# Another order table for a scan-plus-MLP kernel on one core: same operations, other turns, 39 table loads instead of 43

## The chip, the core and the metric

The kernel runs on one core of a Trainium2 chip. A core has five engines that each work through their own list of instructions in order: TensorE (PE in the rows; PEld are its weight loads), VectorE (DVE), ScalarE (ACT), GpSimd (POOL) and SyncE (SP), which here only issues DMAs. They wait for each other through semaphores. The metric is the device time of one execution in microseconds (us); lower is better. The median of three runs before the change is 571.08 us.

## The reference

```
for t in range(S):                                   # S = 768, for 4 x 8 heads, D = 48
    ar, ai = (a_re_n[:, :, t, :, None], a_im_n[:, :, t, :, None])
    new_re = ar * S_re - ai * S_im
    new_im = ar * S_im + ai * S_re
    kv = np.einsum('bhd,bhe->bhde', k[:, :, t], v[:, :, t])
    S_re, S_im = (new_re + kv, new_im)
    y[:, :, t] = np.einsum('bhd,bhde->bhe', q[:, :, t], S_re)
```

Here a_re_n and a_im_n are a_re and a_im, scaled so that their magnitude stays under 0.999. The result y, as 3072 rows of 384, goes through a two-layer MLP: h = x @ w_in (384 to 2048), g = h * tanh(softplus(h)), out = g @ w_out (2048 to 384), all in float32.

## The kernel before

**Tiling.** The 768 time steps of the 4 batches are cut into 12 units of 256 steps, each of two chunks of 128. The recurrence is computed chunk by chunk with matmuls. A unit goes through three stages.

- *Elementwise* (`ew_steps`): magnitudes and phases of the decay, with logarithm, exponential, sine and arctangent on ACT, scans and products on DVE, then `X` and `QK` (the k and q that carry the decay) are sent through DMA into the tile `T`, with head dimensions on the partitions.
- *Attention* (`attn_steps`): for each chunk the masked products of q and k (`amat`: matmuls into `pa` or `pp`, DVE masks them into `am`), the transposed k (`kn`: matmuls into `pkn`, or a DVE transpose and a DMA in later units), the output `yv` (matmuls into `ypsum` from `am` and v, and from `T` and the state `S`) and the new state `upd` (matmuls into `pd` or `pp`, DVE adds and scales into `S`). ACT copies `ypsum` into `y`, and DMAs bring it into `xf`, from which come the high and low parts `xH` and `xL`.
- *MLP* (`moe_steps`): eight steps a unit. `mm1` makes `ph`, 18 matmuls of 256 columns (two halves of nine); then ACT, DVE, ACT, ACT, ACT, DVE turn it into `g`, which is split into `gh` and `gl`; `mm2` adds 12 matmuls of 384 columns to `po`. At the end of a unit DVE scales `po` into `o`, and a DMA writes it out.

Beside these stand the loading and splitting of the weights (`raw`, `wx`, `w`) and 84 matmuls on a constant, `junk` (L516), 40 of which wait for the first phase on DVE and 44 for the first copy of `y`; they compute nothing that is used.

**Column widths.** A matmul of `ph`, `po`, `pa`, `pkn` and `junk` works on the full 128 columns of the array. Those of `ypsum` (L603, 48 output rows) and of `pd` in units 0 to 2 (L623) work in a half of 64 columns, those of `pp` (L583 for the masked products, L623 for the state, from unit 3 on) in a strip of 32. In TensorE's order these widths follow each other in runs; a place where one matmul has another width than the one before it is called a turn here.

**Order.** The code is written once, in a plan of due times; the tables in `ORDER` then fix the order of every engine's instructions. A table lists numbers of instructions in the order in which the code made them; `a+n` stands for n of them from a on. `in_order` chains each engine's instructions by its table. ACT's functions lie in two sets of tables, one for logarithm and exponential ("l"), one for sine and arctangent ("t"); `SETS` lists the loads (L240), which the ACT table then places.

```
    for engine, text in ORDER.items():
        ...
        for run in text.split():
            first, _, count = run.partition("+")
            for n in range(int(first), int(first) + int(count or 1)):
                if last is not None:
                    tc.add_manual_dep(own[n], last.name, order, reason="order of the engine")
                last = own[n]
```

At the end a check value `total` is summed over the partitions by one small matmul, `ptotal` (L809); DVE makes the flag `okay` of it, and every engine reads the flag and, where it is set, skips a general path that this input never takes.

Of the kernel before, what the change touches and what calls it, by code (L numbers as in the profile page):

```python
# [117 lines left out]
    """,  # L118
    "DVE": """
# [51 lines left out]
    """,  # L171
    "Pool": """
        14 3+2 1 16 0 15 2 5+6 55 11+3 17 19 18 20+3 24 23 26 25 27+6 35 33+2 37+2 36 39+2 42 41 43+6 50 49 52 51 54
        53
    """,
    "SP": """
# [12 lines left out]
    """,  # L189
}  # L190

SETS = "l t l t l t l t l t l t l t l t l t l t l t l t l t l t l t l t l t l t l t l t l t l"

# [793 lines left out]
```

## Time and profile before

| What | Value |
|---|---|
| runs | 570.53, 571.08, 571.2 us; median 571.08 |
| the profiled execution's span | 570.8 us |
| PE busy | 545.7 us (96%) |
| DVE busy | 474.2 us (83%) |
| ACT busy | 467.9 us (82%) |
| POOL busy | 43.1 us (8%) |
| chain that ended last, by engine | PE 71%, DVE 11%, ACT 10%, DMA 4% |
| ACT table loads | 43, 1283 ns each |

The span of the profiled execution stands 0.3 us under the median of the runs. Busy shares are averages over the whole span: at the start PE waits for data and DVE works, in the middle both are busy, and after some 300 us DVE and ACT have idle time while PE has none. Matmuls are pipelined, so that one is shown with some 0.28 us while the next one starts after 0.12; what a matmul takes of PE's time is the distance from its start to the next one's.

### The profile page before, as it was taken

How to read it: one execution, taken by the hardware profiler on the slowest of the kernel's cores; microseconds unless marked ns; L12 is line 12 of the kernel's file. 1: busy time of each engine (PE TensorE's matmuls, PEld its weight loads, DVE VectorE, ACT ScalarE, POOL GpSimd, SP SyncE). 2: the span in 40 equal slices, each digit the busy share in tenths (PEclk: the TensorE clock that was granted, in tenths of full speed). 3: DMA queues.
4: the chain of work that ended last, by engine and by line, in shares of the span. 5: the costliest groups of instructions: out<-in, count | busy, mean ns of one | idle time of the engine just before them, and what ended most of it. 6: DMA issues, size and time to landing. Idle time of an engine off the chain costs nothing.

```text
span 570.8 us, 14397 instructions
## 1 busy us (share of the span) xinstructions
PE 545.7 (96%) x5830; PEld 507.6 (89%) x5830; DVE 474.2 (83%) x793; ACT 467.9 (82%) x749; POOL 43.1 (8%) x59
## 2 busy tenths in 40 slices
PE   0789999999999999999999999999999999999996
PEld 0367777789999999999999999999999999999996
DVE  5989999999999998989887999886799787545543
ACT  7889899799979898998988997798987967545671
POOL 4021313431000000000000010000000000000000
PEclk9979999999999999999999999999999999999999
DMA  8666874815563755705647508617524615201001
GB/s 297 218 174 217 279 248 139 265 51 149 164 174 108 218 178 144 211 16 166 170 133 208 161 21 220 199 34 191 160 73 130 210 51 149 75 7 53 1 15 45
DMA packets 69063, 81.65 MB, mean 143 GB/s; under 512 B 6144, under 2 KB 60672, under 8 KB 68992
## 3 DMA queue, kind: packets, MB, share of 16 engines
q1 hardware_dynamic: 68992, 80.68, 48.0%
q8 instruction: 47, 0.77, 0.5%
q14 instruction: 24, 0.20, 0.1%
HBM read 45.51 MB, written 11.40 MB: 100 GB/s over the span
## 4 chain that ended last, share of the span: by engine, by line
PE 71%; DVE 11%; ACT 10%; DMA 4%; issue 2%; SPq 1%; DVEq 0%; ACTq 0%
PE ph L690 27%; PE po L727 27%; PE ypsum L603 6%; PE pp L583 3%; ACT L240 2%; PE po L723 2%; PE pp L623 2%; PE junk L516 2%; DMA T<-QK 1%; DVE X L419 1%; DVE g L700 1%; DMA raw<-w_in 1%; PE ph L686 1%; ACT e L697 1%; ACT e L694 1%
## 5 line engine op out<-in xcount | busy, mean ns | idle before, releaser
L690 PE MATMUL ph<-xH,w 128*128 128x256 f32 x1104 | 215.7, 286 | 0.1
L727 PE MATMUL po<-w,gh 128*128 128x384 f32 x704 | 193.0, 338 | 0.0
L690 PEld LDWEIGHTS ph<-xH,w 128*128 128x128 f32 x1104 | 177.4, 191 | 3.3 <-issue 1.2
L690 PE MATMUL ph<-xL,w 128*128 128x256 f32 x552 | 156.5, 284 | 0.0
L727 PEld LDWEIGHTS po<-w,gh 128*128 128x128 f32 x704 | 127.4, 188 | 1.2 <-issue 0.6
L727 PE MATMUL po<-w,gl 128*128 128x384 f32 x352 | 118.1, 337 | 0.0
L690 PEld LDWEIGHTS ph<-xL,w 128*128 128x128 f32 x552 | 105.2, 191 | 0.9 <-DVE xL L249 0.2
L700 DVE SCALAR_TENSOR_TENSOR g<-e,ph 128x512 f32<-128x512 f32 (+1 forms) x100 | 65.7, 659 | 32.2 <-ACT e L698 31.0
L696 ACT ACTIVATE e<-e 128x512 f32<-128x512 f32 (+1 forms) x100 | 60.7, 610 | 38.5 <-DVE e L695 38.2
L694 ACT ACTIVATE e<-ph 128x512 f32<-128x512 f32 (+1 forms) x100 | 57.1, 574 | 28.9 <-PE ph L690 17.1
L727 PEld LDWEIGHTS po<-w,gl 128*128 128x128 f32 x352 | 66.1, 188 | 0.1
L249 DVE TENSOR_TENSOR gl<-g,gh 128x512 fp32r<-128x512 f32 x88 | 60.1, 685 | 6.9 <-ACT gh L248 6.4
L695 DVE TENSOR_SCALAR e<-e 128x512 f32<-128x512 f32 (+1 forms) x100 | 40.9, 411 | 28.7 <-ACT e L694 28.5
L698 ACT ACTIVATE e<-e 128x512 f32<-128x512 f32 (+1 forms) x100 | 61.0, 612 | 1.8
L697 ACT ACTIVATE e<-e 128x512 f32<-128x512 f32 (+1 forms) x100 | 60.9, 612 | 1.8
L240 ACT ACT_TABLE_LOAD x43 | 55.2, 1283 | 1.5 <-PEq L941 0.8
L516 PE MATMUL junk<-cmask 128*128 128x512 bf16 x84 | 24.9, 445 | 14.4 <-DVE I L425 14.4
L283 POOL TENSOR_TENSOR raw<-raw 128x768 int32<-128x768 int32 x16 | 27.8, 1747 | 84.4 <-DVE raw L281 37.7
L603 PE MATMUL ypsum<-T,S 96*48 96x128 f32 x320 | 32.1, 276 | 0.2 <-DVE S L631 0.2
L516 PEld LDWEIGHTS <-cmask 128*128 128x128 bf16 x84 | 9.1, 111 | 25.8 <-issue 20.6
L248 ACT CAST gh<-g 128x512 fp32r<-128x512 f32 x40 | 24.4, 610 | 4.7 <-DVE g L700 2.5
L584 DVE COPY_PREDICATED am<-tmask,pp 128x512 f32<-128x512 uint8 x36 | 26.0, 734 | 1.3 <-PE pp L583 1.2
(101 smaller groups left out, 839.0 us busy)
## 6 DMA issues: line engine op xcount, KB each, us to landing
T<-X SPq DMA_DIRECT2D x72, 129.0 KB, 2.6
T<-QK SPq DMA_DIRECT2D x72, 129.0 KB, 2.6
raw<-w_in SPq DMA_DIRECT2D x8, 768.0 KB, 7.1
raw<-w_out SPq DMA_DIRECT2D x8, 768.0 KB, 7.6
kd<-vx SPq DMA_DIRECT2D x45, 128.0 KB, 2.9
kn<-kd SPq DMA_DIRECT2D x15, 384.0 KB, 3.1
V<-v SPq DMA_DIRECT2D x12, 384.0 KB, 4.6
out_dram<-o SPq DMA_DIRECT2D x24, 192.0 KB, 2.6
```

The source lines that it names most:

```text
L240: nc.scalar.preload_act_table_set({"l": "natural_log_exp_and_others", "t": "trig_and_small"}[name])
L249: leng(out=lo, in0=src, in1=h.bitcast(F32), op=ALU.subtract)
L516: ins = nc.tensor.matmul(junk, cmask, cmask.unsqueeze(1).broadcast_to([P, 4, P]), start=True, stop=True)
L603: nc.tensor.matmul(py[64 * par:64 * par + D, i, :], lhs, rhs, start=n == 0, stop=first or n == 1)
L690: nc.tensor.matmul(ph[:, a, :], rows_in(parts[j][:, wp], kt, a), st[xp][:, kt, :], start=n == 0, stop=n == 8)
L694: act(e, ph, AF.Exp)
L695: nc.vector.tensor_scalar_min(e, e, math.exp(20.0))
L696: act(e, e, AF.Square, bias=1.0)
L697: act(e, e, AF.Ln, scale=0.2, bias=0.2)
L698: act(e, e, AF.Exp, scale=-1.0)
L700: nc.vector.scalar_tensor_tensor(g, e, 2.5, ph, ALU.subtract, ALU.mult)
L727: nc.tensor.matmul(po[t], gp[:, a, tsl], rows_out(parts[NPAIR + j][:, wp], a), start=j in starts and a == 0 and n == 0, stop=j + 1 in ends ...
```

## The change

Only the tables change: the order of the instructions of all five engines (`ORDER`) and the list of table loads (`SETS`), 43 before and 39 after. One line fewer moves every line below by one: L516 is L515 in the changed kernel. Of the tables one line each is shown.

```
 ORDER = {
     "PE": """
-        0+20 48+4 40+4 52+4 20+2 56+4 44+4 60+15 22+13 124+4 75+5 128+2 35 132+4 130 188+6 36+2 226+3 38 80+5 136+4 85
+        0+26 40+4 26+2 48+4 28+2 44+4 30+2 56+4 32+2 52+4 64+16 34 60+4 80+5 35 85 36 86+2 124+8 88+5 132+4 93+2 37
...
-SETS = "l t l t l t l t l t l t l t l t l t l t l t l t l t l t l t l t l t l t l t l t l t l"
+SETS = "l t l t l t l t l t l t l t l t l t l t l t l t l t l t l t l t l t l t l t l"
```

In TensorE's order the number of turns between widths goes from 103 to 97, by kind: wide to narrow (from 128 columns to 64 or 32) 39 and 39, narrow to wide 39 and 38, from 32 to 64 columns 11 and 16, from 64 to 32 columns 14 and 4. Runs of `ph` are now cut at multiples of nine and runs of `po` at multiples of three, and there are more changes between these two, both 128 columns wide: 147 before, 221 after. `ptotal`, before ahead of the last 54 matmuls of `po`, now stands behind them. Of the 84 junk matmuls 20 stood ahead of the first matmul on data, now 26; behind the two runs of `ypsum` of the first chunk stood 62, now 49.

**VectorE, the first chunk.** `am` are the two masked tiles of the first chunk, `S` is the first state, `raw` and `wx` weights; the number behind a name tells tiles apart. Before:

```order
L590 TENSOR_TENSOR am_384<-pa_383,cmask_83 128x512
L397 TENSOR_SCALAR X_296<-X_296 128x3x128 x2
L376 TENSOR_TENSOR I_202<-I_202,X1_295 128x384
L398 SCALAR_TENSOR_TENSOR R_201<-X_296 128x384 x2
L402 SCALAR_TENSOR_TENSOR R_201<-rmask_96,R_201 128x384 x2
L281 SCALAR_TENSOR_TENSOR raw2_170<-raw2_170,wx2_413 128x768
L376 TENSOR_TENSOR I_202<-I_202,X1_295 128x384
L452 TENSOR_SCALAR cnt_234,good_146<-QK_156 128x3
L280 TENSOR_SCALAR wx3_448<-raw3_174 128x768
L628 TENSOR_TENSOR S_428<-pd_429,T_212 96x384
L590 TENSOR_TENSOR am_516<-pa_515,cmask_83 128x512
```

And now:

```order
L589 TENSOR_TENSOR am_380<-pa_379,cmask_83 128x512
L627 TENSOR_TENSOR S_424<-pd_425,T_208 96x384
L396 TENSOR_SCALAR X_292<-X_292 128x3x128
L375 TENSOR_TENSOR I_198<-I_198,X1_291 128x384
L279 TENSOR_SCALAR wx2_409<-raw2_166 128x768
```

The state now follows directly on the second mask; before, eight rows of elementwise and weight work stood between them, and the next chunk's first mask came directly behind the state.

**TensorE, the same place.** `pa` are the products that the masks read, `pkn` the transposed k, `pd` the products that the state reads. Before:

```order
L603 MATMUL ypsum_142<-am_343,V_184 48x128 x4
L552 MATMUL pkn_330<-ident_78,T_212 128x96 x4
L603 MATMUL ypsum_142<-am_384,V_184 48x128 x4
L623 MATMUL pd_429<-V_184,kn_144 64x48
L623 MATMUL pd_429<-V_184,kn_144 33x48
```

And now:

```order
L602 MATMUL ypsum_138<-am_339,V_180 48x128 x4
L515 LDWEIGHTS cmask_83
L515 MATMUL junk_250<-cmask_83 128x512
L515 LDWEIGHTS cmask_83
L515 MATMUL junk_250<-cmask_83 128x512
L587 MATMUL pa_379<-T_208 128x128 x4
L622 MATMUL pd_425<-V_180,kn_140 64x48
```

The matmuls of the state (16, in turns of 64 and 33 output rows) now stand together ahead of the second run of `ypsum`; before, 11 of them stood behind it, and the other five behind 13 junk matmuls and four of `pkn`. ACT's copies of `pkn` into `kn`, which they read, stand ahead of a table load that they followed before.

**TensorE, the first visit to 32 columns (unit 3).** `pp` from `T` are masked products, `pp` from `V,kn` the state's. Before:

```order
L623 MATMUL pp<-V,kn 32x48 x24
L603 MATMUL ypsum<-am,V 48x128
L603 MATMUL ypsum<-am,vx 48x128 x2
L603 MATMUL ypsum<-am,vz 48x128
L603 MATMUL ypsum<-am,V 48x128
L603 MATMUL ypsum<-am,vx 48x128 x2
L603 MATMUL ypsum<-am,vz 48x128
L583 MATMUL pp<-T 32x128 x4
```

And now:

```order
L582 MATMUL pp<-T 32x32 x4
L622 MATMUL pp<-V,kn 32x48 x24
L602 MATMUL ypsum<-am,V 48x128
L602 MATMUL ypsum<-am,vx 48x128 x2
L602 MATMUL ypsum<-am,vz 48x128
L602 MATMUL ypsum<-am,V 48x128
L602 MATMUL ypsum<-am,vx 48x128 x2
L602 MATMUL ypsum<-am,vz 48x128
L726 MATMUL po<-w_1584,gh 128x384
```

The widths of the visit were 128, 32, 64, 32, 128, four turns; now they are 128, 32, 64, 128, three turns.

## Rows read from the trace of the kernel before

**Rows 1.** The page, part 1: busy us (share of the span) and count of instructions.

```profile
PE 545.7 (96%) x5830; PEld 507.6 (89%) x5830; DVE 474.2 (83%) x793; ACT 467.9 (82%) x749; POOL 43.1 (8%) x59
```

**Rows 2.** Busy time by stretch: from:to, length, each engine's busy us (count), granted clock, DMA.

```profile
20.00:40.00 20.00, 14.75 (x111) 9.72 (x110) 17.87 (x38) 16.39 (x30) 3.20 (x2) 0.83 0.72 221
40.00:180.00 140.00, 139.40 (x1271) 120.95 (x1270) 138.80 (x230) 125.81 (x208) 27.78 (x21) 1.00 0.59 182
180.00:556.00 376.00, 375.74 (x4383) 365.34 (x4382) 298.44 (x489) 307.30 (x480) 5.00 (x14) 1.00 0.44 123
```

**Rows 3.** TensorE in order of time: start, us, what, [idle before, releaser]; the start.

```profile
14.36 7.14 PE L516 MATMUL junk<-cmask 128*128 128x512 bf16 x20 [14.36 <-DVE I L425]
24.40 1.13 PE L588 MATMUL pa<-T 96*128 96x128 f32 x8 [2.90 <-DMA T<-QK]
30.62 1.09 PE L603 MATMUL ypsum<-am,V 128*48 128x128 f32 x8 [2.35 <-DVE am L590]
32.89 4.92 PE L516 MATMUL junk<-cmask 128*128 128x512 bf16 x13
38.89 1.05 PE L588 MATMUL pa<-T 96*128 96x128 f32 x8
```

**Rows 4.** VectorE in order of time: second mask, first state, next chunk's first mask.

```profile
29.88 0.69 DVE L590 TENSOR_TENSOR am<-pa,cmask 128x512 f32<-128x512 f32 x1
38.56 0.55 DVE L628 TENSOR_TENSOR S<-pd,T 96x384 f32<-96x384 f32 x1 [1.14 <-PE pd L623]
39.98 0.69 DVE L590 TENSOR_TENSOR am<-pa,cmask 128x512 f32<-128x512 f32 x1 [0.86 <-PE pa L588]
```

**Rows 5.** Busy time by stretch again, from 30 to 36 us.

```profile
30.00:32.00 2.00, 1.38 (x19) 1.36 (x20) 2.00 (x5) 2.00 (x7) 0.00 (x0) 0.51 0.73 195
34.00:36.00 2.00, 2.00 (x6) 0.75 (x5) 2.00 (x6) 2.00 (x4) 0.46 (x1) 0.50 0.36 76
```

**Rows 6.** TensorE in order of time: one visit to 32 columns, and one turn from `ypsum`.

```profile
312.51 0.28 PE L690 MATMUL ph<-xH,w 128*128 128x256 f32 x1
312.72 1.32 PE L583 MATMUL pp<-T 96*32 96x128 f32 x64
313.98 0.39 PE L690 MATMUL ph<-xH,w 128*128 128x256 f32 x1
314.20 0.28 PE L690 MATMUL ph<-xL,w 128*128 128x256 f32 x1
314.32 0.40 PE L690 MATMUL ph<-xH,w 128*128 128x256 f32 x2
...
247.38 0.27 PE L603 MATMUL ypsum<-am,vz 128*48 128x128 f32 x1
247.49 0.27 PE L603 MATMUL ypsum<-am,vz 128*48 128x128 f32 x1
247.69 0.88 PE L623 MATMUL pp<-V,kn 128*32 128x48 f32 x48
```

**Rows 7.** The chain that ended last: start, us, what; one piece of junk at full clock.

```profile
81.73 1.51 PE junk L516 x7
```

**Rows 8.** ScalarE in order of time, the first copies of `kn`.

```profile
27.41 1.28 ACT L240 ACT_TABLE_LOAD   x1
30.79 0.46 ACT L553 COPY kn<-pkn 128x384 f32<-128x384 f32 x1
31.57 0.47 ACT L553 COPY kn<-pkn 128x384 f32<-128x384 f32 x1
```

**Rows 9.** TensorE around `ptotal`, and VectorE's last operation, in order of time.

```profile
556.13 0.34 PE L727 MATMUL po<-w,gh 128*128 128x384 f32 x1
556.40 0.19 PE L809 MATMUL ptotal<-ones,total 128*1 128x1 f32 x2
556.52 0.44 PE L727 MATMUL po<-w,gh 128*128 128x384 f32 x1
...
566.19 0.56 DVE L742 TENSOR_SCALAR o<-po 128x384 f32<-128x384 f32 x1 [0.95 <-PE po L727]
```

More of the change, by code (lines that the diff above doesn't have):

```diff
@@ L75 @@
     "PE": """
[42 rows of a table removed]
[40 rows of a table added]
     """,
     "DVE": """
[26 rows of a table removed]
[26 rows of a table added]
     """,
     "Activation": """
[23 rows of a table removed]
[23 rows of a table added]
     """,
     "Pool": """
-        14 3+2 1 16 0 15 2 5+6 55 11+3 17 19 18 20+3 24 23 26 25 27+6 35 33+2 37+2 36 39+2 42 41 43+6 50 49 52 51 54
-        53
+        3 0 5 14 4 8 16 7 1 13 9 15 2 17 19 18 20 6 21+4 27 26 25 28+2 12 30+2 10 55 33 11 32 34+3 39 37+2 40 42 41 43+2
+        46 45 47+8
     """,
     "SP": """
[12 rows of a table removed]
[13 rows of a table added]
     """,
 }
-SETS = "l t l t l t l t l t l t l t l t l t l t l t l t l t l t l t l t l t l t l t l t l t l"
+SETS = "l t l t l t l t l t l t l t l t l t l t l t l t l t l t l t l t l t l t l t l"
 def in_order(tc, nc):
```

203 rows, old and new, of the table ORDER are left out of this document.

## The prediction, made before the changed kernel ran

> **What bounds the kernel now.** First the busy shares: TensorE 96%, DVE 83%, ACT 82% [rows 1]. The stretches then say where such a mean misleads [rows 2]. From 20 to 40 us TensorE is busy for 14.75 of 20 us: the program starts up and TensorE waits for data. From 40 to 180 us two engines are full at once, TensorE with 139.40 and DVE with 138.80 of 140 us. From 180 to 556 us only TensorE is full (375.74 of 376); DVE idles for 77.6 us there and ACT for 68.7. So after the start there is no gap on TensorE to be closed. The new order can gain in three ways only: less work in TensorE's stream (turns between widths, junk), an earlier start of the unbroken stream, a shorter tail. It can lose wherever it makes TensorE wait, and up to 180 us DVE has nothing in reserve.
>
> Then the start itself. TensorE first runs 20 junk matmuls, gets the first data at 24.40, sits idle for 2.35 us until the second mask is made, and from 30.62 on no longer stops [rows 3]; what it runs then holds 62 of the 84 junk matmuls. 13 of them, at 32.89, take 4.92 us [rows 3], because the granted clock is 0.50 in that stretch, the lower of the two levels [rows 5]; at full clock seven take 1.51 us, 0.216 each [rows 7]. What TensorE works off meanwhile matters to DVE: the state, whose last matmuls stand behind that junk, is made at 38.56 after 1.14 us of DVE idling, and the next chunk's mask at 39.98 after another 0.86 [rows 4]. Those 2.0 us are most of the 3.3 that DVE idles between 20 and 180 us [rows 2].
>
> **Part 1, the turns.** One visit to the 32-column strips gives the price [rows 6]. Into it: the last `ph` starts at 312.51 and the first `pp` at 312.72, 0.21 instead of the 0.12 from one `ph` to the next (314.20 to 314.32), so 0.09. Out of it: the first `ph` starts at 313.98 and the second at 314.20, 0.22 instead of 0.12, so at least 0.10; what the last `pp` adds before the first `ph` can't be told from one row, and I allow another 0.10. Between narrow widths, from 64 to 32: 247.49 to 247.69 is 0.20 instead of 0.11 (247.38 to 247.49), so 0.09. From 32 to 64 no row isolates; I bound it by 0.09 and 0.20, the prices of the other kinds, and take 0.15. The kinds change by 0 (wide to narrow), -1 (narrow to wide), +5 (32 to 64) and -10 (64 to 32): 0 - 0.2 + 0.75 - 0.9 = -0.35 us. `ph` and `po` now alternate 74 times more, 37 pairs. Both are full width, the rows above show no turn there, and at the resolution of these rows a pair costs between 0 and 0.01 us, so 0 to +0.4; I take +0.2. Sum of part 1: -0.2 us, with ends -0.9 (all kinds at 0.15: six turns) and +0.4.
>
> The Trainium skill, "TensorEngine Tiling (Array Packing)", section "Tiling Modes", says that a change of tiling mode drains TensorE. The rows agree that each change costs something; by one price for every switch the six fewer would be worth 0.9 us, by the kinds 0.35.
>
> So the headline of the change is worth next to nothing by itself; it takes away six turns in 103.
>
> **Part 2, the start.** Three moves there work together. On DVE the state follows the second mask at once, where eight rows stood between. On TensorE the state's 16 matmuls stand together, ahead of the second run of `ypsum`. On ACT both copies of `kn`, which these matmuls read, stand ahead of the table load that starts at 27.41; before, the copies ran at 30.79 and 31.57 [rows 8]. So the state can be made when the second mask is, at about 31 instead of 38.56, and DVE neither idles for it (1.14) nor for the mask at 39.98 (0.86): the products for that mask now stand behind 15 junk matmuls, 3.2 us, which end well before DVE has done the elementwise work now put ahead of it. That frees 2.0 us of DVE. Against it, at most 0.4: on ACT the conversion of the first weight now stands ahead of a short logarithm and exponential chain in the first ten microseconds. On SP, two loads of q and k no longer stand between the transfers into the first `T`, and the load of v does not come until after them; the bytes are the same, and I price this at 0, with up to 1 us either way.
>
> TensorE's side allows this gain: 49 instead of 62 junk matmuls behind the second run of `ypsum`, 13 x 0.216 = 2.8 us less work in the unbroken stream. They were idle time in disguise, and now stand ahead, where TensorE waits anyway (the 2.90 and 2.35 us of [rows 3]). But DVE has the last word until 180 us, so that of 2.8 at most 2.0 arrive. And not all of these: I added up, in either order, the durations of DVE's operations (all 793 make 474.2 us [rows 1]) up to the one that TensorE's next matmul needs. Up to 150 us the new order asks for as much as the old one or up to 1.6 us less; at 180 to 200 us for 0.8 to 1.0 us more; from 220 to 340 us for up to 1.9 us more. So some of the 2.0 us go to work that now stands earlier. I take -1.0 us for part 2, with ends 0 and -2.0.
>
> **Part 3, the table loads.** Four loads fewer are 4 x 1.28 = 5.1 us of ACT (one load: [rows 8]). ACT idles for 14.2 of the 140 us up to 180 and 68.7 after [rows 2], so this is off the path: 0. If the cover were gone it would be a gain of up to 5.1; nothing shows ACT as the bound, and I give it no share of the sum.
>
> **Part 4, the tail.** `ptotal` took from the stream 0.10 before it (556.13 to 556.40 instead of 0.17) and 0.12 itself, and its turn back another 0.1 [rows 9]; behind the last `po` it runs beside DVE's last operation at 566.19: -0.3 us. The flag is read after that, beside the last output transfer. The same rows show 4.6 us from the start of DVE's last operation to the end of the span, most of it that transfer, as cover; if the reading does not fit beneath it, up to +1. Also, 54 matmuls of `po` now stand between the last `ph` and the end instead of 69, 15 x 0.17 = 2.6 us less cover for the last step's way through ACT and DVE; I price this at 0, with up to +1. Sum: -0.3, ends -0.5 and +1.5.
>
> Sum: -0.2 - 1.0 - 0.3 = -1.5 us on the 570.8 us of the profiled execution, 569.3; the median stands 0.3 above that span, so **569.6 us**.
>
> **The rivals.** *The start is gained and lost again* (0.22): some other wait takes the place of DVE's 2.0 us, for instance DVE waiting for ACT's sines, whose loads stand elsewhere now. For it: DVE and TensorE are both full to 180 us, and any 1 us of idling on DVE there is 1 us of the end. Against it: the two waits removed make 2.0 of the 3.3 us that DVE idles from 20 to 180 us [rows 2, 4]. Then parts 1 and 4 stay: 571.1 - 0.5 = 570.6, and 570.0 to 571.9 with their ends.
>
> *Slower, because DVE comes later in the middle* (0.23): the 1.9 us more that TensorE's matmuls ask of DVE between 220 and 340 us become waits. It decides from the point where DVE's idle time there is not free but is itself waiting for TensorE and ACT within one step of the MLP; then DVE can't catch up, and TensorE waits. DVE's 77.6 idle us from 180 to 556 [rows 2] speak against it, the fixed order for it. Without the start's gain that is 571.1 - 0.5 + 1.9 = 572.5; if the waits recur in a second stretch, 574.
>
> *The clock stays up* (0.13): TensorE's clock fell after 30 us, when it had been idle for 2.90 and 2.35 us with little between. The new order has six more junk matmuls between the first data matmuls in that stretch and does the state's matmuls earlier. If the level stays at 2.4 GHz, the six us from 30 to 36 at half speed [rows 5] cost up to 3.0 us less; 13 junk matmuls alone show 4.92 - 2.81 = 2.1. DVE must keep up, so I put this at 569.6 - 2.1 = 567.5, down to 566.5.
>
> The Trainium skill, "Perfetto Trace Analysis", section "Matmul Optimizations", says that the matmul engine scales its power with its use, so that matmuls should run back to back; rows 3 and 5 agree in direction, and by it the new order's denser start would be this rival.
>
> **How the numbers follow.** Forecast 0.42 (568.4 to 570.7), start lost 0.22, slower 0.23, clock 0.13. The range for eight in ten takes the clock case from 566.8 on and the slower case up to 573.8. A measurement of this kernel tells 0.2% from no change, 1.1 us: faster is under 569.95, slower above 572.2. Faster: 0.30 of the forecast's 0.42, the clock case 0.13, 0.04 of the lost start: 0.47. Slower: 0.23. The same: 0.30.
>
> **What would show it.** In the new profile: the state on DVE at 31 to 33 us without a wait, and DVE idling under 0.5 us between 30 and 45; the clock in the stretches from 30 to 37 us (0.5 or 1.0); TensorE's last gap of over 1 us ending before 33 us; 13 junk matmuls fewer behind that; TensorE's busy time from 40 to 180 and from 180 to 556 us without new gaps; `ptotal` beside the last output. I am wrong if TensorE's rows show waits for DVE or ACT between 180 and 340 us that add up to over 1 us, or if the start of the unbroken stream does not move and the time falls all the same: then the turns are dearer than the rows say.

## The result: 0.8% slower, and where TensorE now waits

The changed kernel takes 575.78 us (median of four executions, 574.37 to 577.87) beside 571.14 us of the kernel before: a ratio of 1.0082, 95% interval 1.0057 to 1.0107, 4.6 us slower. The forecast was 569.6 and its range ended at 573.8. A second measurement, beside the runs further down, gave 575.75, 1.0088 (1.0074 to 1.0103). The profiled execution took 574.37 us, its span is 572.7; lines stand one lower than before (L589 is the mask, L590 before). Medians below leave out three executions of the last group of runs that were slow as a whole: two of the kernel before (769 and 1362 us) and one of a changed kernel (703 us).

The two profiles lie closer together than the medians: their spans are 570.8 and 572.7, 1.9 us apart instead of 4.6. The changed kernel's profile is the fastest of its first four executions. In every other run here the time is 1.7 to 1.8 us above the span, so the profile of before, with 570.8, belongs to an execution of some 572.5 us, near the slowest of its four (572.42). The traces side by side show less than the whole loss.

First the same views as ahead of the prediction. The page, part 1 (busy us, share, count):

```profile
PE 542.9 (95%) x5830; PEld 504.4 (88%) x5830; DVE 477.4 (83%) x793; ACT 458.7 (80%) x745; POOL 51.4 (9%) x59
```

Busy time by stretch (from:to, length, busy us of PE, PEld, DVE, ACT, POOL, granted clock, DMA):

```profile
20.00:40.00 20.00, 17.30 (x142) 11.39 (x140) 19.80 (x38) 19.01 (x33) 4.35 (x2) 1.00 0.75 236
30.00:32.00 2.00, 0.72 (x9) 0.39 (x8) 1.97 (x5) 2.00 (x6) 0.00 (x0) 1.00 0.56 150
34.00:36.00 2.00, 1.22 (x11) 0.76 (x10) 2.00 (x6) 1.95 (x4) 0.35 (x1) 1.00 0.81 229
40.00:180.00 140.00, 133.89 (x1198) 114.95 (x1198) 138.40 (x225) 122.08 (x203) 34.50 (x27) 1.00 0.60 183
180.00:556.00 376.00, 374.06 (x4408) 364.14 (x4407) 298.15 (x488) 296.31 (x474) 7.28 (x14) 1.00 0.44 123
```

Up to 40 us the change does what was forecast: TensorE has 2.55 us more busy time than in [rows 2], its clock is at 1.00 where it was at 0.50 [rows 5], and DVE idles for 0.2 us. Then it goes wrong: from 40 to 180 us TensorE has 5.5 us less busy time than in [rows 2], while DVE is as full as before (138.40). About half of that is junk that now stands ahead of 40 us, 31 junk matmuls in this stretch instead of 48 (busy time of `junk` alone, before and now):

```profile
40.00:180.00 140.00, 11.84 (x48) 1.00 0.59 182
40.00:180.00 140.00, 9.03 (x31) 1.00 0.60 183
```

That leaves 2.7 us of other work. Behind 180 us TensorE has 1.7 us less.

TensorE in order of time (start, us, what, [idle before, releaser]), up to the second chunk and around 120 us:

```profile
14.75 8.66 PE L515 MATMUL junk<-cmask 128*128 128x512 bf16 x26 [14.75 <-DVE I L424]
32.23 2.33 PE L515 MATMUL junk<-cmask 128*128 128x512 bf16 x10 [1.50 <-ACT y L607]
...
47.93 0.82 PE L515 MATMUL junk<-cmask 128*128 128x512 bf16 x3
48.68 0.43 PE L602 MATMUL ypsum<-am,V 128*48 128x128 f32 x4
...
49.38 0.39 PE L602 MATMUL ypsum<-T,S 96*48 96x128 f32 x4
52.52 0.42 PE L602 MATMUL ypsum<-am,V 128*48 128x128 f32 x4 [2.75 <-DVE am L589]
...
53.22 0.39 PE L602 MATMUL ypsum<-T,S 96*48 96x128 f32 x4
...
119.52 0.39 PE L689 MATMUL ph<-xH,w 128*128 128x256 f32 x1 [0.84 <-DVE g L699]
128.20 0.39 PE L689 MATMUL ph<-xH,w 128*128 128x256 f32 x1 [0.99 <-DVE g L699]
```

The last gap of over 1 us no longer ends at 30.62 [rows 3] but at 52.52. The kernel before had this at the same place:

```profile
48.86 3.19 PE L516 MATMUL junk<-cmask 128*128 128x512 bf16 x14
51.99 0.43 PE L603 MATMUL ypsum<-am,V 128*48 128x128 f32 x4
...
53.57 0.39 PE L603 MATMUL ypsum<-T,S 96*48 96x128 f32 x4
```

Its TensorE ran 14 junk matmuls (48.86) ahead of the second chunk's 32 matmuls of `ypsum`. The changed one has 3 there, does the first 16 and then waits for the mask that the others read. That mask is made at the same time in both, and the last matmuls of `ypsum` start at 53.57 and 53.22. So in this execution, with its clock at 1.00, the wait by itself costs nothing beside the kernel before. TensorE falls behind later, at its waits for g (0.42 at 94.85, then 0.84 and 0.99). The mask and what stands ahead of it, DVE of the kernel before and of the changed kernel, in order of time:

```profile
51.78 0.68 DVE L590 TENSOR_TENSOR am<-pa,cmask 128x512 f32<-128x512 f32 x1
```

```profile
29.32 0.68 DVE L589 TENSOR_TENSOR am<-pa,cmask 128x512 f32<-128x512 f32 x1
29.92 0.54 DVE L627 TENSOR_TENSOR S<-pd,T 96x384 f32<-96x384 f32 x1
...
36.69 2.17 DVE L401 TENSOR_TENSOR_SCAN R<-rmask,R 128x384 f32<-128x384 uint8 x1
38.79 1.36 DVE L415 TENSOR_TENSOR I<-I,X 128x3 f32<-128x3 f32 x1
...
50.43 1.44 DVE L426 COPY ncar<-I 128x3 f32<-128x3 f32 x1
51.79 0.68 DVE L589 TENSOR_TENSOR am<-pa,cmask 128x512 f32<-128x512 f32 x1
```

The state stands at 29.92, without a wait, 8.6 us sooner than in [rows 4]. And yet the mask comes at 51.79. Three rows in between are stretched: the same scan takes 0.96 at 33.96, a COPY of three columns 0.17 at 33.90. What they have in common stands on GpSimd, its 16 integer additions on the weights (L282). The changed kernel's GpSimd in order of time, then the group of these additions (total us, mean ns | idle before) in the changed kernel and the one before:

```profile
35.65 4.48 POOL L282 TENSOR_TENSOR raw<-raw 128x768 int32<-128x768 int32 x2 [23.22 <-ACT raw L277]
49.78 2.07 POOL L282 TENSOR_TENSOR raw<-raw 128x768 int32<-128x768 int32 x1 [9.65 <-issue]
```

```profile
L282 POOL TENSOR_TENSOR raw<-raw 128x768 int32<-128x768 int32 x16 | 36.2, 2265 | 78.9 <-ACT raw L277 30.1 <-DVE raw L280 19.8 <-issue 14.0
```

```profile
L283 POOL TENSOR_TENSOR raw<-raw 128x768 int32<-128x768 int32 x16 | 27.8, 1747 | 84.4 <-DVE raw L281 37.7 <-ACT raw L278 32.7 <-DVE wx L280 7.3
```

All three stretched rows run beside an addition, and the additions themselves are longer. Counted over all of DVE's rows (duration over the median of the same line and shape by more than 0.15 us), there were 6 stretched rows with 4.2 us before and are 10 with 9.0 us now, all beside an addition (the expectation of add8_after, further down, has one row fewer in either kernel). That is how the start was lost by 51.79: DVE no longer idles 2.0 us [rows 4], but up to there three rows lose 3.7 us to GpSimd, where one had lost 1.2.

The Trainium skill, "SBUF — State Buffer", section "Who interferes with whom", says that VectorE shares a pair of SBUF ports with GpSimd, that a VectorE instruction with two inputs in SBUF contends with a GpSimd instruction that reads SBUF, and that a copy, a cast or a tensor_scalar can, in a mode that takes both pairs of ports; there the other engine blocks altogether. The rows agree, also where they show no loss: a mask, whose one input is in PSUM, ran in 0.68 us beside an addition, and the scan behind it was stretched from 0.95.

```profile
110.94 0.68 DVE L589 TENSOR_TENSOR am<-pa,cmask 128x512 f32<-128x512 f32 x1
111.54 1.30 DVE L418 TENSOR_TENSOR_SCAN X<-rmask,I 128x384 f32<-128x384 uint8 x1
```

### The profile page after: what moved, and what is told of

Read it like the earlier page. It is cut to its first block, busy times and chain, and to the rows that moved or that the text cites. A ratio compares the mean times of both kernels' runs of the same rounds, so it can differ in the third digit from the quotient of the medians.

```text
span 572.7 us, 14403 instructions
## 1 busy us (share of the span) xinstructions
PE 542.9 (95%) x5830; PEld 504.4 (88%) x5830; DVE 477.4 (83%) x793; ACT 458.7 (80%) x745; POOL 51.4 (9%) x59
## 4 chain that ended last, share of the span: by engine, by line
PE 61%; DVE 17%; ACT 10%; DMA 6%; issue 4%; SPq 2%; DVEq 0%; ACTq 0%
PE po L726 27%; PE ph L689 26%; PE ypsum L602 4%; PE pp L582 3%; DMA raw<-w_in 2%; DVE g L699 2%; ACT L239 2%; SPq L461 2%; DVE e L694 1%; PE pp L622 1%; DVE raw L280 1%; DVE X L418 1%; DVE w L248 1%; ACT e L696 1%; ACT e L697 1%
## 5 line engine op out<-in xcount | busy, mean ns | idle before, releaser
L689 PE MATMUL ph<-xH,w 128*128 128x256 f32 x1104 | 225.0, 287 | 1.8 <-DVE g L699 1.8
L726 PE MATMUL po<-w,gh 128*128 128x384 f32 x704 | 202.8, 339 | 0.3 <-DVE o L739 0.2
L689 PEld LDWEIGHTS ph<-xH,w 128*128 128x128 f32 x1104 | 180.7, 190 | 5.4 <-DVE g L699 3.4
L726 PEld LDWEIGHTS po<-w,gh 128*128 128x128 f32 x704 | 129.6, 188 | 3.4 <-issue 2.0
L694 DVE TENSOR_SCALAR e<-e 128x512 f32<-128x512 f32 (+1 forms) x100 | 43.0, 433 | 29.4 <-ACT e L693 28.9
L282 POOL TENSOR_TENSOR raw<-raw 128x768 int32<-128x768 int32 x16 | 36.2, 2265 | 78.9 <-ACT raw L277 30.1
L515 PE MATMUL junk<-cmask 128*128 128x512 bf16 x84 | 24.9, 421 | 16.3 <-DVE I L424 14.7
L515 PEld LDWEIGHTS <-cmask 128*128 128x128 bf16 x84 | 8.3, 106 | 25.0 <-issue 19.3
L582 PEld LDWEIGHTS pp<-T 96*32 96x32 f32 x1152 | 23.4, 109 | 7.0 <-issue 2.5
```

The costliest lines, as they stand in the source:

```text
L582: nc.tensor.matmul(pa[row:row + 32, i, t0:], T[:, 1, s0:s0 + 32], T[:, 0, t0:C], start=True, stop=True)
L689: nc.tensor.matmul(ph[:, a, :], rows_in(parts[j][:, wp], kt, a), st[xp][:, kt, :], start=n == 0, stop=n == 8)
L694: nc.vector.tensor_scalar_min(e, e, math.exp(20.0))
L726: nc.tensor.matmul(po[t], gp[:, a, tsl], rows_out(parts[NPAIR + j][:, wp], a), start=j in starts and a == 0 and n == 0, stop=j + 1 in ends ...
```

## Experiments

Two theories stood at the beginning. *Collisions*: DVE is held up beside GpSimd's additions. *Order*: DVE's new order puts other work ahead of the masks and g. All runs below are compared with the kernel before on the same chip (571.2 to 571.4).

**Where the loss lies.** The two orders were joined at 180 us, by what had started until then; each engine's list goes on with the rest of the other order.

```
 s_after_180:  changed order | 180 us | order of before   (SETS: 43 loads)
 s_before_180: order of before | 180 us | changed order   (SETS: 39 loads)
```

> The changed order up to 180 us (everything that had started by then in the changed kernel's trace), behind it the rest in the order of before, with before's 43 table loads. Theory 'early': the loss of 4.6 us lies ahead of 180 us, where the changed kernel's TensorE has 133.9 of 140 us busy instead of 139.4: 573.5 to 575.5. Theory 'late': the loss comes from the orders behind 180 us, where TensorE has 374.1 of 376 instead of 375.7: 571 to 572.

> The order of before up to 180 us, behind it the rest in the changed order, with 39 table loads. Theory 'early': only the 1.7 us of waits behind 180 us are left, less 0.5 for turns and tail: 571 to 572.5. Theory 'late': 574 to 576.

Measured: s_after_180 578.31 (1.0106, 1.0084 to 1.0128), s_before_180 570.46 (0.9985, 0.9975 to 0.9994). The loss lies ahead of 180 us; behind it the changed order even gains 0.75 us, where the expectation still had a loss. s_before_180 is the best kernel of this study that leaves nothing out, if only by 0.15%. The median of s_after_180 is 2.5 us above the changed kernel's, more than expected (the two intervals overlap), and its trace shows a second cause (TensorE's wait, then by stretch, as above):

```profile
53.44 0.42 PE L602 MATMUL ypsum<-am,V 128*48 128x128 f32 x4 [2.76 <-DVE am L589]
```

```profile
52.00:56.00 4.00, 2.56 (x24) 2.02 (x25) 4.00 (x11) 0.38 (x1) 1.01 (x2) 0.83 0.82 208
56.00:60.00 4.00, 4.00 (x21) 3.78 (x20) 3.99 (x7) 3.96 (x8) 2.19 (x1) 0.50 0.88 237
60.00:64.00 4.00, 4.00 (x34) 3.12 (x34) 3.26 (x7) 3.59 (x6) 0.00 (x0) 0.82 1.01 318
```

After the wait for the mask TensorE's clock was at the lower level, 0.50 (1.2 of 2.4 GHz), and the matmuls that ran there were real work. The profiled execution of the changed kernel shows no such fall, but its other executions may have it: of its ten executions those with a mean granted clock of 0.999 or 1.0 took 572.96, 573.19, 574.37 and 575.43, those with 0.991 to 0.997 took 575.61 to 577.87, 2.5 us more in the mean. Where the clock fell in these is not recorded. A low mean alone says little: 87 of 91 executions of the kernel before, beside these runs, lie between 0.991 and 0.998, and in its trace the clock falls at 30 us [rows 5].

**Short additions.**

```
-        nc.gpsimd.tensor_tensor(hi, hi, lo, ALU.add)
+        nc.gpsimd.tensor_tensor(hi[:, :8], hi[:, :8], lo[:, :8], ALU.add)
```

> The changed kernel, but each of GpSimd's 16 integer additions on the weights works on 8 of its 768 columns; the low halves of the other columns are left out of the weights. Theory 'collisions': VectorE is held up beside these additions, in the changed kernel nine operations by 7.8 us together, before five by 3.5 us, and this is where the time went: 569 to 571.5, within 1.5 us of the kernel before with the same edit. Theory 'order': VectorE is asked for other work ahead of the masks and g, whatever GpSimd does: 572.5 to 575, still 3 us or more above the kernel before with the same edit.

> The kernel before, but each of GpSimd's 16 integer additions on the weights works on 8 of its 768 columns. Both theories: 568 to 570.5, since 3.5 us of VectorE's time beside these additions go, of which TensorE can take less than all. What tells them apart is the distance to the changed kernel with the same edit: under 1.5 us for 'collisions', 3 us or more for 'order'.

Measured: add8_after 571.26 (0.9995, 0.9980 to 1.0010), add8_before 570.55 (0.9983, 0.9974 to 0.9993). The edit takes 4.5 us off the changed kernel and 0.7 off the one before; of the distance of 4.6 us 0.7 are left, which is within the noise (the intervals of the two ratios overlap). DVE of add8_after shows why, with the three rows at their usual length and the mask 3.5 us sooner; TensorE's waits of 40 to 180 us follow (engine line <- releaser: us, times, longest):

```profile
36.13 0.93 DVE L401 TENSOR_TENSOR_SCAN R<-rmask,R 128x384 f32<-128x384 uint8 x1
36.98 0.14 DVE L415 TENSOR_TENSOR I<-I,X 128x3 f32<-128x3 f32 x1
...
48.18 0.18 DVE L426 COPY ncar<-I 128x3 f32<-128x3 f32 x1
48.27 0.68 DVE L589 TENSOR_TENSOR am<-pa,cmask 128x512 f32<-128x512 f32 x1
```

```profile
PE pkn L551 <- DMA T<-QK: 1.7, 1, 1.7
PE pa L587 <- ACT kn L552: 0.2, 1, 0.2
PE po L722 <- DVE g L699: 0.2, 1, 0.2
```

The waits for the mask (2.75) and for g (0.84, 0.99) are gone.

**Is it the port or the time that the addition takes?** Short additions also make the weights ready sooner.

```
+        nc.gpsimd.tensor_tensor(hi[:, :8], hi[:, :8], lo[:, :8], ALU.add)
+        nc.gpsimd.tensor_tensor(lo[:, 8:], hi[:, 8:], lo[:, 8:], ALU.add)   # read by nobody
```

> The changed kernel; each of GpSimd's 16 additions on the weights works on 8 columns, as before, and is followed by a second one on the other 760 columns whose result goes into words that nobody reads (so the low halves of those columns are left out of the weights). The next step of the weights waits only for the short one. Theory 'collisions' (VectorE is held up while GpSimd runs a long addition): the loss comes back, 573.5 to 577. Theory 'latency' (the short additions helped because the weights were ready sooner): it stays away, 569 to 572.5.

Measured: 573.73 (1.0050, 1.0030 to 1.0069): 2.5 of the 4.5 us come back through additions whose result nobody waits for, though the next short addition stands behind them on GpSimd and comes later than in add8_after. In its profile DVE's stretched rows have 7.9 us instead of 9.0 and meet the additions at other places (the mask comes at 50.27), so the rest may be fewer meetings or the sooner weights; that isn't separated.

**Moving two rows.** Two of the 16 rows of DVE that release an addition were put ahead of rows that read PSUM.

```
 L426 COPY ncar<-I                                -L280 raw7 (behind six rows)
 L417 SCALAR_TENSOR_TENSOR I<-ncar,I               L279 TENSOR_SCALAR wx7
+L280 SCALAR_TENSOR_TENSOR raw3 (was 3 sooner)    +L280 SCALAR_TENSOR_TENSOR raw7
 L589 TENSOR_TENSOR am<-pa,cmask                   L699 SCALAR_TENSOR_TENSOR g x2
```

> The changed kernel, nothing left out; in VectorE's order two of the 16 rows that release an addition (L280 of raw3 and raw7) stand elsewhere by 3 and 6 places, so that masks, states and g, which read one operand from PSUM, follow the release instead of a COPY and a TENSOR_SCALAR within SBUF, which were held up by 1.28 and 1.27 us. Theory 'collisions': both stretched rows go, 2.5 us less of VectorE and 1 to 3 us less in all: 573 to 575 beside 576. Theory 'order': a mask comes 0.2 to 0.9 us later, so the same or up to 1 us more: 576 to 577.

> The changed kernel unedited, as the measure beside which the three others of this group stand. 574 to 578 by either theory.

Measured: after_again 575.75, two_moved 575.90 (1.0074, 1.0058 to 1.0090), no gain. The first move did its part (wait at the mask 1.81 instead of 2.75 us). The second put a collision at a worse place: the released row now itself ran into the addition before it, ahead of two g's, and TensorE, which had not waited there, waited 1.67 us. DVE, then TensorE of this kernel:

```profile
101.80 2.11 DVE L280 SCALAR_TENSOR_TENSOR raw<-raw,wx 128x768 uint32<-128x768 uint32 x1
103.83 1.27 DVE L699 SCALAR_TENSOR_TENSOR g<-e,ph 128x512 f32<-128x512 f32 x2
```

```profile
104.56 4.13 PE L722 MATMUL po<-raw,g 128*128 128x384 f32 x7 [1.67 <-DVE g L699]
```

The stretched rows still sum to 8.1 us (9.0 in the changed kernel). Both rows that were to be spared are at their usual length, but others are stretched that had met no addition, such as a state at 67.48 by 1.3 us. A move of a few places changes the meetings that come behind it.

**The new start alone.**

```
 s_after_start: changed order | 40.5 us | order of before   (SETS: 43 loads)
```

> The changed order up to 40.5 us (the new start, with the state directly behind the second mask), behind it the rest in the order of before, with 43 table loads. If the new start is worth what it gives TensorE there, 2.0 us or more, and the loss comes from other meetings of VectorE and GpSimd behind it: 568 to 570. If the start is gained and lost again in VectorE's first fifty us: 570.5 to 572. If the order of before, shifted against its additions, meets them as badly as the changed one: 573 to 577.

Measured: 572.76 (1.0018, 1.0010 to 1.0027), between the second and the third range: the start is no gain, even with the order of before behind it. TensorE, and the stretches around:

```profile
51.98 0.67 PE L602 MATMUL ypsum<-am,V 128*48 128x128 f32 x4 [3.72 <-DVE am L589]
```

```profile
48.00:52.00 4.00, 0.28 (x8) 0.03 (x3) 4.00 (x6) 3.94 (x8) 1.41 (x1) 0.76 0.47 124
52.00:56.00 4.00, 4.00 (x27) 3.63 (x28) 4.00 (x8) 0.72 (x2) 0.93 (x2) 0.50 0.86 267
```

TensorE gets to the mask sooner, stands 3.72 us, and then works at half clock. DVE sets the time there, as the prediction said, and what TensorE saved earlier it pays back at the lower clock.

**Junk back into the wait.** If that is right, junk matmuls ahead of the mask must help, though they add work to the busiest engine.

```
-WREP, WREP2, WK = 40, 44, -9.4
+WREP, WREP2, WK = 40, 56, -9.4      # start_junk15: 59; all new ones ahead of the second chunk's ypsum
```

> The changed kernel with 12 more junk matmuls (96 instead of 84), all directly ahead of the second chunk's ypsum, where TensorE waited 2.75 us for a mask with 3 junk there (the kernel before has 14 there). Theory 'clock': that idle stretch lets TensorE's clock fall in a part of the executions; ten executions so far with a mean granted clock of 0.997 to 0.991 or of 0.999 to 1.0 lie at 575.6 to 577.9 and at 573.0 to 575.4. Filled, the fall there goes and the slower group with it: median 573 to 574.5. Theory 'late': only VectorE's lateness counts, and junk in a wait changes nothing: 575 to 577.

> The changed order up to 40.5 us and the order of before behind it (572.8 without more junk; TensorE waited 3.72 us for that mask and its clock was at 0.50 from 52 to 56 us), with 15 more junk matmuls directly ahead of the second chunk's ypsum. Theory 'clock': no fall, some 7 us at half speed less: 569.5 to 571.3. Theory 'late': 572.3 to 573.3.

Measured: after_junk12 573.74 (1.0042, 1.0029 to 1.0055), 2.0 us under the changed kernel, all five executions between 573.20 and 575.46 at 0.999 or 1.0; start_junk15 571.88 (1.0010, 1.0001 to 1.0018), 0.9 under s_after_start. *Clock* is borne out for the changed kernel: the median is that of the unedited executions that kept the clock (572.96 to 575.43). For the start alone the measured time lies between the two theories, the 0.9 us are within the noise, and with the clock kept (0.997 to 1.0) the new start is still no better than the kernel before. The stretches of after_junk12, where TensorE had 1.77 of 4 us in the changed kernel:

```profile
48.00:52.00 4.00, 4.00 (x31) 2.04 (x29) 4.00 (x5) 2.84 (x5) 2.32 (x2) 1.00 0.67 177
```

Two more kernels of this group missed their numbers.

> The changed kernel with 10 more junk matmuls ahead of the second chunk's ypsum, and in VectorE's order the one row of raw3 (L280) moved by 3 places, so that no COPY meets GpSimd's addition: the mask comes 1 us sooner. If clock and collision are two causes that add: 572 to 573.5, 0.5 to 1.5 us under the kernel with junk alone. If the second gives nothing: the same as with junk alone.

> The changed order up to 40.5 us, the order of before up to 180 us, the changed order behind it, and 15 more junk matmuls ahead of the second chunk's ypsum. If the start is worth something once the clock is kept, and the changed order behind 180 us is worth the 0.7 us that it gave behind the order of before (570.46 beside 571.21): 568.5 to 570.5. If the start gives nothing: 570.5 to 571.5.

moved_junk10 took 575.22 (1.0070, 1.0053 to 1.0087): with one row moved the stretched rows again sum to 8.9 us (9.3 in after_junk12), 3.0 of them between 60 and 80 us where there had been 1.9, and TensorE waits 1.7 us for a transfer into `xf` at 63.68 that it had not waited for. three_junk15 took 572.52 (1.0026, 1.0014 to 1.0038), 2.1 us above s_before_180; TensorE waits for transfers into `T` at narrow visits there (2.3 us, beside 1.2 in s_before_180), which accounts for about half of that.

**What is left, and whether the causes add.** With the junk the changed kernel is still 2.5 us above the one before.

```
 add8_junk12        = after_junk12 + additions on 8 columns
 later_junk12       = after_junk12 + three visits to 32 columns 9 to 12 matmuls later
 add8_later_junk12  = both
 later_before180    = s_before_180 + the three visits later
```

> The changed kernel with 12 more junk matmuls at the mask (573.74) and GpSimd's additions on 8 of 768 columns (the low halves of the other columns are left out of the weights). What is left of the loss, 2.5 us, is either 'collisions' (TensorE's waits for g at 58, 94, 118 and 127 us, 2.6 us together: they go, 570.3 to 571.5) or 'transfers' (TensorE's waits for T at four narrow visits behind 180 us, 3.0 us together: they stay, 572.8 to 574).

> The changed kernel with 12 more junk matmuls at the mask (573.74); three visits to 32 columns whose first matmul waited for a transfer into T (at 232, 271 and 485 us) stand 9 to 12 matmuls later in TensorE's order, 1.1 to 1.6 us. Theory 'transfers': these waits go, 1.0 to 2.6 us: 571.1 to 572.8. Theory 'collisions': the wait is only put off to the mask and ypsum behind the visit, or the engines catch up there anyway: 573 to 574.5.

> All three together: 12 more junk, additions on 8 columns, three visits later. If the three causes are separate and all of the loss: 568.5 to 570, under the kernel before with short additions (570.55). If one of them only covers another: as the better of the two single edits, 571 or more.

> The order of before up to 180 us and the changed one behind it (570.46 beside 571.21 of the kernel before), with the three visits later. Theory 'transfers': 0.4 to 1.2 us of waits less: 569.3 to 570.1, and under both kernels. Otherwise 570.3 to 571.

Measured: add8_junk12 570.44 (0.9981, 0.9967 to 0.9995), later_junk12 574.13 (1.0052, 1.0035 to 1.0068), add8_later_junk12 569.78 (0.9979, 0.9961 to 0.9997), later_before180 571.01 (0.9991, 0.9978 to 1.0004). What was left goes with the short additions, 3.3 us. Moving the visits gives nothing that can be told from the noise, alone or on top of the short additions; in later_junk12 the wait is put off. TensorE of later_junk12, 40 to 560 us:

```profile
PE ph L689 <- DVE g L699: 2.8, 3, 1.0
PE po L722 <- DVE g L699: 0.4, 1, 0.4
```

Two of the three waits for g are the old ones at 118 and 127 us; the third is new, at 232 us, where the visit had stood.

With short additions and with junk the changed kernel (570.44) stands where the kernel before stands with short additions (570.55). The two causes together are the loss: junk alone brings 2.0 us, short additions alone 4.5, both 5.3, so they overlap. That fits, since the wait for the mask goes with short additions too. The 0.8 us that junk brings on top of them are within the noise; in the profile of add8_after the clock still falls, at 54.8 us, behind a wait of 1.7 us for a transfer.

## Why the prediction was wrong

**The failed step is part 2, the start**, and in it the price of DVE's operations. The prediction added up their durations from the trace of before, in the new order, and took these for fixed. They aren't: a row that meets one of GpSimd's additions is up to 1.3 us longer. The trace of before showed it, in two rows of DVE whose like take 0.55 (the rows of the kernel before, in order of time):

```profile
35.65 1.78 DVE L280 TENSOR_SCALAR wx<-raw 128x768 uint32<-128x768 uint32 x1
57.01 1.84 DVE L280 TENSOR_SCALAR wx<-raw 128x768 uint32<-128x768 uint32 x1
```

But GpSimd, busy 8% [rows 1], was not read as an engine that could cost DVE anything, and the change shifted its 16 additions against DVE's rows. The term was -1.0 with ends 0 and -2.0; no end above 0 was given. What the runs show in its place is some +5.3 us ahead of 180 us (575.78 beside 570.46 of s_before_180, which has the old order there).

**The second mistake is in the same part**: the 13 junk matmuls fewer behind the first chunk were booked as idle time in disguise that had moved ahead. They were, but disguised idle time held the clock. The kernel before had 14 of them ahead of the mask at 51.78, where TensorE would have waited for DVE; the new table left 3. The rival *the clock stays up* came true where it was looked for (1.00 from 30 to 36 us) and was worth nothing: there the kernel before had run junk at half speed, and start_junk15, whose clock stayed up, is no faster than it. In six of ten executions the mean clock was lower all the same, and where a profile of a joined order caught the fall (s_after_180, s_after_start) the low clock met the matmuls behind the wait for that mask, real work. It cost 2.0 us by after_junk12; the rival had -2.1.

**Right in direction, wrong in place and size**: *the start is gained and lost again* is what happened up to 51.79, through collisions and not through the sines. *DVE comes later* happened too, but at 50, 118 and 127 us and not from 220 to 340; the slower case ended at 574 and did not count on the clock. Between 180 and 340 us, where the prediction set its sign of being wrong, TensorE's waits for DVE and ACT come to 0.5 us; the signs that failed are the last gap of over 1 us (52.52 instead of before 33) and the busy time from 40 to 180 us.

**What held.** DVE has the last word up to 180 us: 138.40 of 140 us, and nothing that TensorE gained ahead of 50 us arrived. Parts 1 and 4 together were -0.5; s_before_180, which has the changed order only behind 180 us, shows -0.75 (-1.4 to -0.3), so they fit, though turns and tail weren't measured apart. Part 4's cover held: DVE's last `o` starts at 568.31, 4.4 us ahead of the end, beside 4.6 [rows 9]. Part 3: four loads fewer, ACT 9.2 us less busy, and no wait of TensorE names a load; no run tested it alone.

**Slips in the working that change nothing.** The 0.3 us added to the span rest on a wrong pairing: the profile was of an execution of some 572.5 us. Taken from the median of 571.08 the -1.5 us give 569.6 all the same. The ends of parts 1 and 4 sum to -1.4 and +1.9, so the first rival's 570.0 to 571.9 is narrower than they make it (569.7 to 573.0). The 0.4 us set against part 2's gain have no row.

**Open.** How much of the 4.5 us that short additions bring is due to the sooner weights (add_unused leaves 2.0 unexplained), and why the waits behind 180 us differ from execution to execution (1.9 us in the changed kernel's profile, 0.7 in that of its second measurement).

## What to carry to other kernels

Where a reordering keeps every operation, the durations still move: list the rows of VectorE that are longer than others of their shape, see what GpSimd ran beside them, and count those meetings anew in the new order. Filler on an engine that must wait in any case is not waste; before taking it away, look at where the next wait is and what the clock does there. And a saving on one engine ahead of a stretch that another engine sets is worth nothing until that other engine's time has been followed up to the next place where the two meet.

## What the runs showed of the hardware

An integer addition of 128x768 on GpSimd takes 1.46 us at its shortest (35.54 in the kernel before), and 5.03 us at one place of the changed kernel, where VectorE runs rows one behind the other, most of them with two inputs in SBUF or a tensor_scalar within it:

```profile
63.70 5.03 POOL L282 TENSOR_TENSOR raw<-raw 128x768 int32<-128x768 int32 x1 [4.67 <-ACT raw L277]
```

None of VectorE's rows from 63.58 to 68.33 is stretched, so it was GpSimd that waited, through several of them. At 50.43 it was VectorE that waited, between two rows, and a COPY of three columns took 1.44 us. An addition of 8 columns took 1.13 us at one place and 0.20 at another (add_unused):

```profile
35.74 1.13 POOL L282 TENSOR_TENSOR raw<-raw 128x8 int32<-128x8 int32 x1 [23.16 <-ACT raw L277]
38.94 0.20 POOL L282 TENSOR_TENSOR raw<-raw 128x8 int32<-128x8 int32 x1
```

The section of the Trainium skill named above ("SBUF — State Buffer", "Who interferes with whom") says that whoever issues first gets the shared ports for its whole instruction. By the 5.03 us the one who waits is not always next in turn when that instruction ends; spans on GpSimd are rough in this profile, and no run tested the order of turns.

TensorE idled 2.75 us ahead of the same mask in three traces with the same order up to there. In two, the changed kernel's, its clock stayed at 1.00; in the third, s_after_180, it fell, and stood at 0.50 for some 7 us (worked out from the granted clocks of its three stretches above).
